# Eight PSUM banks in one rotation for two middle batches, and a new order of their output products and transpositions

## The chip, the cores and the metric

The kernel runs on one core of a Trainium2 chip. The metric is the time of one execution in microseconds on the device. The engines named below are TensorE (PE in the rows, PEld for its weight loads), VectorE (DVE), ScalarE (ACT), GpSimd (POOL) and the queue of DMA issues (SP).

## The reference

Three layers run one after another on 4 batches of 576 positions, all in fp32: windowed attention with 8 heads of 64, a gated MLP in which the gate mixes positions, and a gated convolutional MLP.

```python
scores = scale * q @ k.T;  scores = where(mask, scores + bias, -1e9)   # window of 128
attn = exp(scores - max);  x = (attn / sum(attn)) @ v                  # per head, then [B, S, 512]

h = gelu(x @ w_in);  u, v = split(h)
v_n = (v - mean(v)) / sqrt(var(v) + 1e-6) * g_ln
v_s = einsum('ts,bsd->btd', w_sg, v_n) + b_sg[:, None]
x = x + (u * v_s) @ w_out

h = relu(x @ w_in2);  conv = 3-tap convolution of h along the positions
out = (h * sigmoid(conv)) @ w_out2
```

## The kernel before

The whole kernel is one program in which every engine has its own queue and takes its instructions strictly in the order in which they stand there. `_steps()` writes the order of the work by hand as a list of short names, each one a step of one batch; a scheduler then places the instructions of these steps on the engines, mostly in that order, but it may move one up or down by its own estimate of time.

Attention for batch b + 1 is woven into the gated MLP of batch b. Attention works on pairs of heads, four to a batch (pair 1 of batch 2 is `2.1`). Its steps:

- `L`, `M` load a pair's k and q, and its v. `C` (line 464) computes the scores: 23 groups of matmuls into five PSUM banks named `sc`, and nine masking instructions on VectorE (line 451) that read them.
- `E` (line 489) is nine exponentials on ScalarE, and `N` (line 495) divides by the sums: nine multiplications, shared between VectorE and GpSimd (line 242).
- `T` (line 529) turns the weights with 13 transpositions into four banks named `pT`; four copies to SBUF (`ph`) follow, two on ScalarE and two on VectorE. The first transposition waits for the last masking instruction listed before it (line 533).
- `A` (line 585) forms the pair's products with v in two banks named `o`, 52 small matmuls. The first waits for all four copies (`s["waits"]`, line 538). `X` splits the result x into a high and a low part (`xg`).

The gated MLP's steps each take one bank: `V` (`psv`, line 746, five a batch), `U` (`psu`, line 787), `G` (`pss`, line 824) and `W` (`pso`, line 845). `U`, `G`, `W` are named by batch, half (256 or 320 positions) and a quarter of the columns. A `G` step goes on as: VectorE scales it (line 840), GpSimd multiplies by u, a copy makes the high part `gh`, a subtraction the low part `gl`. A `W` step is 12 matmuls over `gh` and `gl` of all four quarters; VectorE adds x (line 858) and a DMA writes the result. Steps `a` (line 382) narrow a piece of a later layer's weights: five instructions on VectorE that write `wa` (lines 324 to 331), two on GpSimd, and DMAs in and out.

PSUM has eight banks. Line 276 divides them:

```python
psum(net=2, att=6)
```

`bank(name)` (line 265) takes the next of two banks for names that begin with ps, and the next of six for the others. When a pool's banks are used up, the next step waits until the oldest tile of that pool has been read. The step `B` (line 866) makes one pool of all eight; the kernel before never runs it. Before batch 3 line 895 sets `psum(net=4)`.

Of the kernel before, what the change touches and what calls it, by code (L numbers as in the profile page):

```python
# [14 lines left out]
B, H, S, D = 4, 8, 576, 64  # L15
# [38 lines left out]
def _steps():  # L54


    def of(p):
        return f"{p // NP}.{p % NP}"

    def scores(p):  # L60
        return [f"C{of(p)}"]

    def weigh(p):
        return [f"E{of(p)}", f"N{of(p)}"]

    def back(p):
        return [f"T{of(p)}", f"A{of(p)}"]

    def halves(p):
        return [f"X{of(p)}.0", f"X{of(p)}.1"]  # L70

    def loads(p):
        return [f"L{of(p)}", f"M{of(p)}"]

    weave = lambda main, more: [
        x for i, m in enumerate(main) for x in [m] + more[i * len(more) // len(main) : (i + 1) * len(more) // len(main)]
    ]
    put_by = [f"a{i}.{c}" for i in (1, 0) for c in range(16)]
    s = """
        l0.0 k0 l1.0 k5 l2.0 l3.0 v0.0 v1.0 v2.0 v3.0 j1.0 j1.1 l0.1  # L80
        c0.0 e0.0 c1.0 e1.0 n0.0 c2.0 e2.0 t0.0 n1.0 c3.0 e3.0 l1.1 j1.2 j1.3 v0.1 i1.0 z0.0 X0.0.0 t1.0 n2.0 z1.0 X0.1.0
        l2.1 v1.1 i1.1 t2.0 n3.0 z2.0 X0.2.0 c0.1 e0.1 l3.1 j0.0 i1.2 t3.0 z3.0 X0.3.0 c1.1 e1.1 v2.1 i1.3 n0.1 c2.1 j0.1 v3.1 j0.2 t0.1 e2.1 n1.1 z0.1
        i0.0 c3.1 e3.1 j0.3 i0.1 k4 V0.0 t1.1 n2.1 z1.1 V0.1 t2.1 n3.1 z2.1 i0.2 U0.0.0 i0.3 t3.1 z3.1 X0.0.1 U0.0.1
        X0.1.1 U0.0.2 X0.2.1 X0.3.1
    """.split()
    for b in range(B - 1):
        p = NP * (b + 1)
        V = [f"V{b}.{j}" for j in range(5)]
        U = [[f"U{b}.{half}.{m}" for m in range(4)] for half in range(2)]
        G = [[f"G{b}.{half}.{m}" for m in range(4)] for half in range(2)]  # L90
        W = [[f"W{b}.{half}.{m}" for m in range(4)] for half in range(2)]
        if b == 0:
            uv = ["g0", "g1", V[2], "g2", "o0.0", U[0][3], "g3", "o0.1", V[4]] + loads(p) + ["g4", "o1.0"] + scores(p) + ["o1.1", V[3], "o2.0", "o2.1"]
            uv += loads(p + 1) + U[1][:2] + ["o3.0"] + scores(p + 1) + ["o3.1"] + loads(p + 2) + U[1][2:] + scores(p + 2)
        else:
            uv = V[:2] + loads(p) + scores(p) + V[2:] + loads(p + 1) + scores(p + 1) + U[0] + loads(p + 2) + U[1][:1] + scores(p + 2) + U[1][1:]
        T, A = ([f"{x}{of(p + i)}" for i in range(4)] for x in "TA")
        gw = weigh(p) + G[0] + weigh(p + 1) + G[1][:1] + loads(p + 3) + T[:1] + G[1][1:2] + W[0][:1] + A[:1] + halves(p)
        gw += weigh(p + 2) + W[0][1:2] + T[1:2] + W[0][2:] + A[1:2] + scores(p + 3) + halves(p + 1) + weigh(p + 3) + T[2:3] + G[1][2:3]
        gw += A[2:3] + halves(p + 2) + G[1][3:] + T[3:] + W[1][:1] + A[3:] + halves(p + 3) + W[1][1:]  # L100
        if b == 0:
            s += uv + gw
        else:
            now = put_by[10 * b - 10 : 10 * b]
            s += weave(uv, now[:4]) + weave(gw, now[4:])
    first = " ".join(s)
    n = [f"V3.{j}" for j in (0, 1, 2, 4, 3)] + [f"U3.{half}.{m}" for half in range(2) for m in range(4)]
    n += [f"G3.0.{m}" for m in range(4)] + ["G3.1.0"] + [f"W3.0.{m}" for m in range(4)]
    n += [f"G3.1.{m}" for m in range(1, 4)] + [f"W3.1.{m}" for m in range(4)]

    for m in range(4):
        n[n.index(f"U3.{m % 2}.{m // 2 + 1}")] += f" w0.{m // 2}.{m % 2}"
    n[n.index("W3.0.3")] += " y0.0"
    n[n.index("G3.1.2")] += " y0.1"
    n[n.index("W3.1.0")] += " y0.2"
    n[n.index("W3.1.1")] += " y0.3"
    s = weave(n[:-6], put_by[LATE:]) + n[-6:]
    late = [f"w1.{k}.{h}" for k in range(4) for h in range(2)]
    s = s[:-6] + weave(s[-6:], late)
    second = " ".join(["x0.0.1.2.3"] + s)  # L120
    return first, second


STEPS = _steps() + (
    """
    D0.0 D0.1 D0.2 D0.3 x1.0.1 D0.4 x1.2.3 D0.5 y1.0 D0.6 y1.1 D0.7 y1.2 y1.3 D1.0 D1.1 F0.0 D1.2 D1.3 F0.1 D1.4
# [989 lines left out]
```

## Time and profile before

| | us |
|---|---|
| median of 3 runs | 545.88 (544.20 to 546.34) |
| the profiled execution | 545.05 |
| its span | 543.2 |
| TensorE busy in the span | 522.3 (96%) |
| VectorE, ScalarE, GpSimd busy | 370.0 (68%), 258.6 (48%), 243.0 (45%) |
| batch 1 of the gated MLP (`V1.0` to the end of `W1.1.3`) | 126.10 to 205.50 |
| batch 2 | 205.50 to 284.91 |

The span begins with the first instruction and ends with the last; 1.85 us of the profiled execution lie around it. In a list in order of time, successive instructions of one kind are merged into one row, and the brackets at its end give the idle time before it and what ended it. [...]

### The profile page before, as it was taken

The page shows a single profiled execution, that of the slowest core. Times are in us where ns is not written, and L with a number is a line of the kernel's source. Part 1 is how long each engine was busy: PE and PEld are TensorE (multiplying, and loading weights), DVE is VectorE, ACT ScalarE, POOL GpSimd, SP SyncE. Part 2 cuts the span into 40 slices and gives each one's busy share as a digit, 9 for nine tenths or more (in the row PEclk, how much of TensorE's full clock was granted, in tenths as well). Part 3 has the DMA queues.
Part 4 walks back from the last instruction along what each step waited for, and adds up shares of the span by engine and source line. Part 5 has one row for each costly group of instructions (what it writes and reads, how often), then busy time and mean ns, then how long its engine had stood idle before and what let it go on. Part 6 is the DMA issues. An engine that isn't in the chain of part 4 may idle for free.

```text
span 543.2 us, 11985 instructions
## 1 busy us (share of the span) xinstructions
PE 522.3 (96%) x4548; PEld 474.8 (87%) x4548; DVE 370.0 (68%) x959; ACT 258.6 (48%) x673; POOL 243.0 (45%) x383
## 2 busy tenths in 40 slices
PE   8997989999999999999999999999999999999997
PEld 6776879898898888898988999998998999999887
DVE  4999898754869865869867788698467344654300
ACT  6694578342458451457544534453444334444311
POOL 2444249552246263237363354245586445465500
PEclk9999989999999999999999999999999999999999
DMA  8974441433260766240734424811202200100111
GB/s 298 385 241 172 150 126 45 146 120 106 80 194 21 229 183 198 68 136 24 241 124 131 154 80 155 306 43 43 83 21 69 77 21 19 42 21 22 37 39 59
DMA packets 33209, 63.93 MB, mean 118 GB/s; under 512 B 3968, under 2 KB 13952, under 8 KB 33152
## 3 DMA queue, kind: packets, MB, share of 16 engines
q1 hardware_dynamic: 33008, 63.04, 35.0%
q8 instruction: 36, 0.59, 0.4%
q14 instruction: 21, 0.17, 0.1%
q10 hardware_dynamic: 144, 0.13, 0.1%
HBM read 48.47 MB, written 14.68 MB: 116 GB/s over the span
## 4 chain that ended last, share of the span: by engine, by line
PE 57%; DVE 17%; ACT 11%; POOL 8%; DMA 3%; issue 3%; ACTq 0%; POOLq 0%; DVEq 0%; SPq 0%
PE psg L213 31%; PE pso L213 7%; PE psu L213 5%; ACT t L186 5%; PE psv L213 4%; PE o L213 3%; PE sc L213 3%; POOL t L242 3%; PE pss L213 3%; DVE t L451 2%; PE pT L515 2%; DMA x2d<-x 2%; DVE t L242 1%; DVE wa L330 1%; DVE wa L329 1%
## 5 line engine op out<-in xcount | busy, mean ns | idle before, releaser
L213 PEld LDWEIGHTS psg<-x2g,w 128*128 128x128 f32 x768 | 103.2, 188 | 2.4 <-ACT hb L970 0.7
L213 PE MATMUL psg<-x2g,w 128*128 128x256 f32 (+1 forms) x768 | 104.7, 294 | 0.6 <-ACT hb L970 0.5
L213 PE MATMUL psg<-wout,gh 128*128 128x512 f32 (+1 forms) x272 | 80.1, 378 | 0.0
L186 ACT ACTIVATE t<-t,st 128x192 f32<-128x192 f32 (+1 forms) x144 | 61.9, 431 | 16.6 <-DVE st L451 16.6
L213 PE MATMUL pss<-wsg,vn 128*128 128x256 f32 (+1 forms) x448 | 63.6, 299 | 0.3 <-DVE t L840 0.2
L213 PEld LDWEIGHTS pss<-wsg,vn 128*128 128x128 f32 x448 | 60.7, 191 | 1.2 <-DVE t L840 1.1
L974 DVE SCALAR_TENSOR_TENSOR cc<-hb,cw,cc 128x576 f32<-128x576 f32 x32 | 26.5, 832 | 47.0 <-POOL cc L242 47.0
L213 PEld LDWEIGHTS psg<-wout,gh 128*128 128x128 f32 x272 | 49.7, 188 | 8.7
L213 PE MATMUL psu<-xg,win 128*128 128x320 f32 (+1 forms) x384 | 54.4, 298 | 3.0 <-ACT win L222 1.7
L213 PEld LDWEIGHTS psu<-xg,win 128*128 128x128 f32 x384 | 51.6, 188 | 4.3 <-ACT win L222 1.8
L213 PE MATMUL pso<-gh,wo 128*128 128x256 f32 (+1 forms) x256 | 52.2, 300 | 1.7 <-DVE t L840 1.6
L213 PE MATMUL psg<-wout,gl 128*128 128x512 f32 (+1 forms) x136 | 50.9, 378 | 0.0
L213 PE MATMUL psv<-win,xg 128*128 128x512 f32 x192 | 47.6, 398 | 1.0 <-DVE wa L328 0.9
L242 POOL TENSOR_SCALAR cc<-hb,cw 128x576 f32<-128x576 f32 x32 | 28.4, 889 | 42.7 <-ACT hb L970 42.7
L451 DVE CUSTOM_DVE_ANT_0 t<-sc,tab 128x192 f32<-128x192 f32 (+1 forms) x144 | 40.3, 335 | 4.9 <-PE sc L213 4.9
L970 ACT ACTIVATE hb<-psg 128x576 f32<-128x576 f32 x32 | 20.7, 651 | 47.5 <-PE psg L213 45.1
L213 PEld LDWEIGHTS pso<-gh,wo 128*128 128x128 f32 x256 | 40.2, 188 | 3.4 <-DVE t L840 2.8
L213 PEld LDWEIGHTS psv<-win,xg 128*128 128x128 f32 x192 | 35.4, 188 | 8.9 <-ACT win L222 1.0
L231 DVE TENSOR_TENSOR gg<-cc,hb 128x576 f32<-128x576 f32 x32 | 30.2, 944 | 17.2 <-ACT cc L186 17.0
L213 PE MATMUL pso<-gl,wo 128*128 128x256 f32 (+1 forms) x128 | 36.9, 301 | 2.4 <-DVE gl L231 1.7
L231 POOL TENSOR_TENSOR t<-t,u 128x256 f32<-128x256 f32 (+1 forms) x32 | 27.0, 850 | 21.3 <-DVE t L840 20.3
L231 POOL TENSOR_TENSOR gl<-gg,gh 128x512 fp32r<-128x512 f32 x24 | 33.7, 1406 | 0.6
(101 smaller groups left out, 963.1 us busy)
## 6 DMA issues: line engine op xcount, KB each, us to landing
V<-in_v_dram SPq DMA_DIRECT2D x12, 704.0 KB, 5.1
x2s<-x2d SPq DMA_DIRECT2D x16, 288.0 KB, 2.9
w<-in_w_in_dram SPq DMA_DIRECT2D x8, 512.0 KB, 7.4
w<-in_w_out_dram SPq DMA_DIRECT2D x16, 256.0 KB, 2.9
w<-in_w_in_dram SPq DMA_DIRECT2D x16, 256.0 KB, 2.7
wout<-w2d SPq DMA_DIRECT2D x8, 512.0 KB, 6.1
q<-in_q_dram SPq DMA_DIRECT2D x12, 320.0 KB, 3.9
out_dram<-ot SPq DMA_DIRECT2D x15, 256.0 KB, 2.0
```

Source lines behind the costliest of these rows:

```text
L186: ins = nc.scalar.activation(*args, **kw)
L213: return nc.tensor.matmul(out, lhsT, rhs, start=start, stop=stop, **kw)
L231: return (nc.vector if eng == "dve" else nc.gpsimd).tensor_tensor(dst, a, b, op=op)
L242: e.tensor_scalar(dst, src, col, 1.0, op0=ALU.mult, op1=ALU.mult)
L329: nc.vector.tensor_scalar(a, a, 0x07FFFFFF, 3, op0=ALU.bitwise_and, op1=ALU.logical_shift_left)
L330: nc.vector.scalar_tensor_tensor(a, high, 0xC0000000, a, op0=ALU.bitwise_and, op1=ALU.bitwise_or)
L451: nc.vector.tensor_tensor_reduce(e, bank, table, scale=-SCALE, scalar=3e38, op0=ALU.add, op1=ALU.min, accum_out=mx)
L515: grouped(nc.tensor.transpose(ps[:, i * P : (i + 1) * P], src, ident), first and i == 0, waits if i == 0 else ())
L970: nc.scalar.activation(h[:, 1 : S + 1], ps[:, 256 : 256 + S], AF.Relu)
L974: nc.vector.scalar_tensor_tensor(cc, h[:, 0:S], cw[:, 0, c : c + 1], cc, op0=ALU.mult, op1=ALU.add)
```

## The change

After batch 0 the new step `B` joins the eight banks into one rotation, which serves attention and gated MLP alike in batches 1 and 2. In these two batches the list is also new from the exponentials on: the first output product `W.0.0` stands behind the first pair's `A` and `X` and the third pair's `E` and `N`; the third pair's transposition `T` stands ahead of the fourth pair's scores `C`; the last two products `G.1.2` and `G.1.3` and the fourth `W.0.3` come together behind the fourth pair's `E` and `N`.

```diff
--- before.py
+++ after.py
@@ -98,8 +98,12 @@
         gw = weigh(p) + G[0] + weigh(p + 1) + G[1][:1] + loads(p + 3) + T[:1] + G[1][1:2] + W[0][:1] + A[:1] + halves(p)
         gw += weigh(p + 2) + W[0][1:2] + T[1:2] + W[0][2:] + A[1:2] + scores(p + 3) + halves(p + 1) + weigh(p + 3) + T[2:3] + G[1][2:3]
         gw += A[2:3] + halves(p + 2) + G[1][3:] + T[3:] + W[1][:1] + A[3:] + halves(p + 3) + W[1][1:]
+        if b:
+            gw = weigh(p) + G[0] + weigh(p + 1) + G[1][:1] + loads(p + 3) + T[:1] + G[1][1:2] + A[:1] + halves(p)
+            gw += weigh(p + 2) + W[0][:1] + T[1:2] + W[0][1:2] + A[1:2] + halves(p + 1) + T[2:3] + W[0][2:3] + scores(p + 3)
+            gw += A[2:3] + halves(p + 2) + weigh(p + 3) + G[1][2:] + W[0][3:] + T[3:] + W[1][:1] + A[3:] + halves(p + 3) + W[1][1:]
         if b == 0:
-            s += uv + gw
+            s += uv + gw + ["B"]
         else:
             now = put_by[10 * b - 10 : 10 * b]
             s += weave(uv, now[:4]) + weave(gw, now[4:])
```

On TensorE the first place is the end of the last early product of the mixing matrix in batch 1. Before:

```order
L213 MATMUL pss_2547<-wsg0_851,vn_2065 128x320
L213 MATMUL pss_2547<-wsg0_851,vn_2095 128x320
L213 MATMUL pss_2547<-wsg1_852,vn_2095 128x320
L213 MATMUL pso_2569<-gh_2390,wo_891 128x256 x2
L213 MATMUL pso_2569<-gl_2391,wo_891 128x256
```

and now:

```order
L217 MATMUL pss_2552<-wsg0_851,vn_2070 128x320
L217 MATMUL pss_2552<-wsg0_851,vn_2100 128x320
L217 MATMUL pss_2552<-wsg1_852,vn_2100 128x320
L217 MATMUL o_2575<-ph_2549,V_1979 64x64 x4
L217 MATMUL o_2575<-ph_2542,V_1979 64x192
```

The 18 first matmuls of the two output products `pso` are gone from here; the first pair's products with v (`o`) follow `pss` directly.

The second place is behind these products, around the second pair's transposition. Before:

```order
L213 MATMUL o_2596<-ph_2537,V_1974 64x64
L213 MATMUL o_2596<-ph_2530,V_1974 64x64
L515 MATMUL pT_2672<-ident_80,t0_85 128x128 x4
L515 MATMUL pT_2679<-ident_80,t0_85 128x128 x4
L515 MATMUL pT_2686<-ident_80,t0_85 128x128 x4
L515 MATMUL pT_2693<-ident_80,t0_85 128x128
L213 MATMUL pso_2569<-gh_2456,wo_891 128x256 x2
L213 MATMUL pso_2569<-gl_2457,wo_891 128x256
```

and now:

```order
L217 MATMUL o_2585<-ph_2542,V_1979 64x64
L217 MATMUL o_2585<-ph_2535,V_1979 64x64
L217 MATMUL pso_2645<-gh_2395,wo_891 128x256
L519 MATMUL pT_2661<-ident_80,t0_85 128x128 x4
L519 MATMUL pT_2668<-ident_80,t0_85 128x128 x4
L519 MATMUL pT_2675<-ident_80,t0_85 128x128 x4
L519 MATMUL pT_2682<-ident_80,t0_85 128x128
L217 MATMUL pso_2645<-gh_2395,wo_891 128x256
```

One matmul of the first output product stands ahead of the transposition, and all others behind it.

On VectorE the place is in batch 2, between the third pair's division by the sums and the copies of the second pair's transposed weights (`ph`). Before:

```order
L242 TENSOR_SCALAR t2_87<-t2_87,r_3834 128x192 x4
L231 TENSOR_TENSOR gl_3647<-t1_3643,gh_3646 128x256
L224 CAST gh_3702<-t1_3699 128x320
L231 TENSOR_TENSOR xg_3819<-x_3775,xg_3819 128x256
L224 COPY ph_3863<-pT_3862 128x512
L224 COPY ph_3870<-pT_3869 128x512
L231 TENSOR_TENSOR xg_3822<-x_3775,xg_3822 128x320
```

and now:

```order
L246 TENSOR_SCALAR t2_87<-t2_87,r_3823 128x192 x4
L235 TENSOR_TENSOR gl_3652<-t1_3648,gh_3651 128x256
L228 CAST gh_3707<-t1_3704 128x320
L235 TENSOR_TENSOR xg_3795<-x_3764,xg_3795 128x256
L328 TENSOR_SCALAR wa_3800<-w64_3798 128x256
L332 TENSOR_SCALAR wa_3800<-wa_3800 128x256
L333 TENSOR_SCALAR wa_3800<-wa_3800 128x256
L334 SCALAR_TENSOR_TENSOR wa_3800<-w64_3798,wa_3800 128x256
L335 SCALAR_TENSOR_TENSOR wa_3800<-w64_3798,wa_3800 128x256
L235 TENSOR_TENSOR xg_3811<-x_3764,xg_3811 128x320
L228 COPY ph_3852<-pT_3851 128x512
L228 COPY ph_3859<-pT_3858 128x512
```

Five instructions of a narrowing step (`wa`) and both low parts of x (`xg`) now stand ahead of the two copies; before, one low part did. In batch 1 three of the five stand there.

## Rows read from the trace of the kernel before

**Rows 1.** Busy time by engine, two stretches (columns: length, busy us, instructions, clock, DMA)

```profile
169.79:205.50 35.71, 32.69 (x419) 30.38 (x418) 27.50 (x85) 17.46 (x53) 17.23 (x33) 1.00 0.59 180
...
250.40:284.91 34.51, 32.46 (x419) 30.46 (x418) 27.50 (x85) 17.48 (x53) 17.20 (x33) 1.00 0.47 151
```

**Rows 2.** TensorE in order of time, batch 1 (columns: start us, us, engine, line, operation)

```profile
169.79 0.41 PE L213 MATMUL pso<-gh,wo 128*128 128x256 f32 x2
...
173.44 2.05 PE L213 MATMUL o<-ph,V 128*64 128x64 f32 x52
...
175.41 1.64 PE L515 MATMUL pT<-ident,t 128*128 128x128 f32 x13
...
176.81 0.48 PE L213 MATMUL pso<-gh,wo 128*128 128x256 f32 x2
...
177.96 2.04 PE L213 MATMUL o<-ph,V 128*64 128x64 f32 x52 [0.21 <-ACT ph L222]
...
179.94 0.50 PE L213 MATMUL pso<-gh,wo 128*128 128x256 f32 x2
...
182.88 1.97 PE L213 MATMUL sc<-k,q 64*64 64x128 f32 x46
...
184.64 4.37 PE L213 MATMUL pss<-wsg,vn 128*128 128x320 f32 x28
...
201.89 0.55 PE L213 MATMUL pso<-gh,wo 128*128 128x320 f32 x2
```

**Rows 3.** TensorE in order of time, batch 2

```profile
205.50 5.68 PE L213 MATMUL psv<-win,xg 128*128 128x512 f32 x24
...
219.00 2.09 PE L213 MATMUL psv<-win,xt 128*128 128x512 f32 x8 [0.43 <-ACT v L186]
...
226.17 4.76 PE L213 MATMUL psu<-xg,win 128*128 128x256 f32 x36 [0.45 <-ACT u L186]
...
250.40 0.40 PE L213 MATMUL pso<-gh,wo 128*128 128x256 f32 x2
...
284.91 8.40 PE L213 MATMUL psv<-win,xg 128*128 128x512 f32 x36
```

**Rows 4.** ScalarE in order of time, first pair's copies in batches 1 and 2

```profile
171.14 1.04 ACT L222 COPY ph<-pT 128x512 f32<-128x512 f32 x2
...
251.76 1.05 ACT L222 COPY ph<-pT 128x512 f32<-128x512 f32 x2
```

**Rows 5.** VectorE in order of time, batches 1 and 2

```profile
172.38 1.07 DVE L330 SCALAR_TENSOR_TENSOR wa<-w,wa 128x256 uint32<-128x256 uint32 x1
...
197.52 1.02 DVE L231 TENSOR_TENSOR gl<-t,gh 128x320 fp32r<-128x320 f32 x1 [2.68 <-ACT gh L222]
...
237.86 0.29 DVE L324 TENSOR_SCALAR wa<-w 128x256 uint32<-128x256 uint32 x1
...
239.30 0.42 DVE L331 SCALAR_TENSOR_TENSOR wa<-w,wa 128x256 uint32<-128x256 uint32 x1
...
254.45 1.59 DVE L242 TENSOR_SCALAR t<-t,r 128x192 f32<-128x192 f32 x4
...
257.20 1.28 DVE L224 COPY ph<-pT 128x512 f32<-128x512 f32 x2
```

**Rows 6.** GpSimd in order of time, batch 1

```profile
172.30 0.88 POOL L231 TENSOR_TENSOR t<-t,u 128x320 f32<-128x320 f32 x1 [2.05 <-DVE t L840]
...
191.62 3.71 POOL L242 TENSOR_SCALAR t<-t,r 128x128 f32<-128x128 f32 x8 [0.73 <-DVE r L499]
```

**Rows 7.** TensorE in order of time, the wait before 76.79

```profile
76.79 2.20 PE L213 MATMUL sc<-k,q 64*64 64x192 f32 x24 [2.08 <-DVE st L451]
```

**Rows 8.** Busy time by engine in two-microsecond stretches behind that wait

```profile
76.00:78.00 2.00, 1.21 (x23) 1.13 (x23) 2.00 (x15) 2.00 (x10) 0.00 (x0) 0.79 0.75 291
...
78.00:80.00 2.00, 2.00 (x10) 2.00 (x9) 1.97 (x8) 2.00 (x10) 0.14 (x1) 0.50 0.04 8
...
80.00:82.00 2.00, 2.00 (x17) 2.00 (x16) 2.00 (x17) 2.00 (x10) 1.35 (x2) 0.86 0.82 240
```

## The prediction

> **What bounds the kernel now.** I read the busy shares first. TensorE works 96% of the span, so only its waits can be won. The change touches batches 1 and 2, and in each the list is new only behind the six early `pss` products, from 169.79 to 205.50 and from 250.40 to 284.91. [...]
>
> Then I took TensorE in order of time and worked out what each kind of work takes from start to start [rows 2]: a pair's products with v 1.97 us (173.44 to 175.41), its transpositions 1.40 (175.41 to 176.81), 24 `pso` matmuls of 256 columns 2.94 (179.94 to 182.88), so 0.1225 each and 1.47 for a step of 12, the scores 1.76 (182.88 to 184.64), two `pss` steps 4.37 by their own row; 24 `pso` matmuls of 320 columns from 201.89 to `psv` at 205.50 [rows 2, 3] 3.61, so 0.150 each. The stretch holds 4 products with v, 3 transpositions, 4 + 4 `pso` steps, one set of scores and two `pss` steps: 7.88 + 4.20 + 5.88 + 7.22 + 1.76 + 4.37 = 31.31 us. So before waits 4.4 us in batch 1 and 3.2 in batch 2, with the pipeline's small gaps in it. This is nearly all the change can win.
>
> **The change part by part.** The work itself stays: the same matmuls, copies and DMAs. What moves is order and banks.
>
> *Banks in the steps V and U.* In batch 1 TensorE does not wait for a bank there. In batch 2 it waits 0.43 us at 219.00 for an activation that reads `psv` and 0.45 at 226.17 for one that reads `psu` [rows 3], each the tile two before in a pool of two. In a rotation of eight the tile before was read long ago. These 0.88 us go, and ScalarE's chain of exponentials starts as much earlier, because it hangs on the last `psu`. Bounds: 0, if VectorE, whose order is unchanged, holds the later steps back, and 0.88. I take 0.88, since ScalarE's copies set the next start.
>
> *The first pair's products ahead of the first `pso`.* Before, 18 `pso` matmuls stand between `pss` and these products. Now nothing does, but the products wait for all four copies of the transposed weights. ScalarE's two stand behind the third pair's exponentials and end at 171.14 + 1.04 = 172.18 and at 251.76 + 1.05 = 252.81 [rows 4]; TensorE can start some 0.1 later, at 172.28 and 252.91. So TensorE stands idle for about 2.5 us, from 169.79 and from 250.40, where before it had `pso` to do. The products begin 1.2 us earlier than before (173.44), but with 18 matmuls (2.2 us) still owed.
>
> *Up to the second pair's products.* Batch 1: 172.28 + 1.97 + 0.12 (one `pso` matmul) + 1.40 = 175.77; the other 23 take 2.82, to 178.59. Then the second pair's products wait for copies on VectorE. In batch 2 that queue reads, before: four normalizations (from 254.45, 1.59, to 256.04), 1.16 us for a low part, a cast and a subtraction, then the two copies from 257.20 for 1.28 [rows 5]. Now a fifth normalization of 128 columns stands there (an estimate of 0.3, from 1.59 / 4 for 192), and behind the same 1.16 come five narrowing instructions (237.86 to 239.30 + 0.42, so 1.86 [rows 5]) and the second low part of x (an estimate of 0.39, a third of the 1.16). The copies end at 256.34 + 1.16 + 1.86 + 0.39 + 1.28 = 261.03, and TensorE starts at 261.1. It was ready at 252.91 + 1.97 + 0.12 + 1.40 + 22 x 0.1225 = 259.1, so it waits 2.0. In batch 1 (80.6 us earlier) three of the five stand in front, 1.12 us: copies end at 179.65, products start at 179.75, a wait of 1.16. At this point the new order has done the same work as before but stands at 179.75 where before stood at 177.96 [rows 2].
>
> What hides beside a neighbour is not certain here. A narrowing instruction took 1.07 us at 172.38 instead of 0.42 while GpSimd multiplied from 172.30 for 0.88 [rows 5, 6]. So each batch's queue may be 0.65 later where such a pair meets, which I keep for the range. [...]
>
> *Scores and third transposition.* The third pair's transposition now stands ahead of the fourth pair's scores and so no longer waits for their masking. Batch 1 goes on without a wait: 179.75 + 1.97 + 1.40 + 1.47 + 1.76 + 1.97 = 188.32, where the two `pss` steps start; they end 4.37 later, at 192.69. Batch 2: 261.1 + 1.97 + 1.40 + 13 x 0.1225 + 1.76 + 1.97 = 269.79, and 274.16.
>
> *The last products.* The `pso` steps of the second half need the low part of the fourth `pss`. Before, the two `pss` steps ended at 184.64 + 4.37 = 189.01 [rows 2], and this low part at 197.52 + 1.02 = 198.54 [rows 5]: 9.53 us for scaling, multiplication, cast and subtraction, of which GpSimd's eight normalizations took 3.71 [rows 6]. Now they stand ahead of that multiplication on GpSimd and mostly beside `pss`. I take 9.53 - 3.71 = 5.82 (bounds: 4.0, as a guess below, since scaling, 0.88 us of multiplication, cast and subtraction must run in turn and two copies stand between, and 9.53). The fourth pair's copies stand just ahead of this subtraction on VectorE, so its products start at 192.69 + 5.82 + 0.1 = 198.6 and, in batch 2, at 280.1. Behind them 37 matmuls of 0.150 are left: 198.6 + 1.97 + 5.55 = 206.1, and 287.6.
>
> So batch 1 ends 0.6 us later than 205.50, batch 2 loses 287.6 - 284.91 = 2.7 less the 0.88. *Banks and queues that cost nothing:* I followed the rotation: each tile eight before is read by then, except the scores of batch 2, whose first bank is freed by an addition behind two copies (0 to 0.35; I take 0). On SP two output writes of a batch come later, and behind them loads of weights that are due 5 us afterwards. Batch 3 and the last layer keep their order up to one `psg` step and are TensorE's.
>
> **Sum.** 545.05 - 0.88 + 0.6 + 2.7 = 547.5 us against the profiled execution's own time, which is 0.83 under the median shown (545.88): 0.3% above that median. I leave the difference between the two out, since the runs spread over 2.1 us. About 0.5% (2.7 us) is what a measurement of this kernel can tell from no change.
>
> **The rivals.**
>
> *The clock falls behind the new waits (slower).* [...] I give this rival 0.27.
>
> *The copies come early after all (faster).* If VectorE's and GpSimd's queues run ahead of my estimates, only the first wait of 2.5 stays, and each stretch takes 31.31 + 2.5 = 33.8: 1.9 and 0.7 less than before, with the 0.88 some 3.5, so 541.6. For it: VectorE has 7 to 8 us free in each stretch [rows 1]. Against it: free time lies elsewhere than ahead of the copies, and the queue is fixed. 0.15.
>
> *The change does not do what it says.* The banks free nothing, since the 0.88 us come back as waits for data, and the moved steps cancel within 1 us: 546.0 to 548.4. 0.10.
>
> **How the numbers follow.** The forecast has 0.48: 547.5, its own range from 543.9 (both last chains at their lower bound, 1.8 less each) to 549.2 (0.65 more for each batch, and the 0.35). Of it 0.10 lie above 548.6 (slower by over 0.5% of the median). With the clock's 0.22 of 0.27 above that and 0.02 of the third, slower is 0.34; faster is 0.14, nearly all from the second rival; within 0.5% is 0.52. The range for 8 in 10 is 543.2 to 550.6.
>
> **What would show it.** In the changed kernel's profile TensorE should stand idle for about 2.5 us ahead of the first `o` in both batches, with ScalarE's copy as what ends it; 1 to 2 us ahead of the second, ended by a copy on VectorE; no wait at the third transposition and none for a bank in batch 2's steps V and U; and some 3 us around the first `pso` step of 320 columns. If the two stretches end under 35 us, my VectorE queue is wrong; if the clock row shows 0.5 there, the first rival is at work.

## The result and the profile after

The changed kernel took 552.35 us (median of 6 runs, 551.47 to 555.08) and the kernel before 546.11 us beside it (6 runs): a ratio of 1.0122 between the means, with a 95% interval of 1.0087 to 1.0158. It is 1.2% slower. The prediction was 547.5 us, with a range up to 550.6; the time lies above it. Medians and ratios here and below leave out a run over 1.5% slower than the fastest of its kernel, which is one run of e17 (558.89 us). The profiled execution of the changed kernel took 554.40 us, its span 552.6.

The first reading compares the kernels by batch. The rows give busy time by engine from the first `psv` of a batch to the first of the next, and for batch 3 to the first `psg` (columns: stretch, its length, then busy us and instructions of PE, PEld, DVE, ACT and POOL, the granted clock, DMA share and GB/s). Before:

```profile
126.10:205.50 79.40, 76.31 (x806) 70.31 (x805) 60.09 (x203) 38.95 (x120) 33.49 (x64) 1.00 0.44 135
205.50:284.91 79.41, 76.41 (x806) 70.20 (x805) 61.68 (x208) 38.84 (x120) 34.55 (x67) 1.00 0.40 127
284.91:334.50 49.59, 49.18 (x333) 46.15 (x331) 39.69 (x93) 20.78 (x49) 20.29 (x31) 1.00 0.42 130
```

After:

```profile
127.07:208.15 81.08, 77.41 (x806) 71.66 (x805) 64.82 (x210) 37.98 (x117) 31.12 (x58) 0.98 0.44 131
208.15:290.62 82.47, 76.22 (x806) 70.21 (x805) 66.61 (x215) 37.87 (x117) 33.28 (x63) 1.00 0.40 122
290.62:343.68 53.06, 49.99 (x332) 46.34 (x331) 39.63 (x92) 20.09 (x47) 20.28 (x32) 1.00 0.40 122
```

Batch 1 lost 1.68 us, batch 2 3.06 and batch 3, whose code did not change, 3.47. Another 0.97 us were lost ahead of batch 1, where both kernels are the same, and 0.22 behind the first `psg`; together 9.40, the difference of the spans. The 0.97 is this execution's own: in e17, the changed kernel once more, batch 1 begins at 125.87 us. VectorE is busy 4.7 to 4.9 us longer in batches 1 and 2, GpSimd 2.4 and 1.3 us less: four of a batch's 36 normalizations went from GpSimd to VectorE.

The stretches of [rows 1], from the end of the six early `pss` products (same columns), and TensorE in them, which answers to [rows 2, 3] (columns: start us, us, engine, line, operation, and in brackets the idle time before it and what ended it):

```profile
170.57:208.15 37.58, 33.91 (x418) 31.89 (x418) 32.43 (x92) 16.68 (x50) 15.08 (x27) 0.95 0.57 168
252.10:290.62 38.52, 32.50 (x418) 30.49 (x418) 32.17 (x92) 16.24 (x48) 15.60 (x28) 1.00 0.44 131
```

```profile
221.06 1.99 PE L217 MATMUL psv<-win,xt 128*128 128x512 f32 x8
...
173.19 3.19 PE L217 MATMUL o<-ph,V 128*64 128x64 f32 x52 [2.62 <-ACT ph L226]
...
181.08 2.04 PE L217 MATMUL o<-ph,V 128*64 128x64 f32 x52
...
189.92 4.38 PE L217 MATMUL pss<-wsg,vn 128*128 128x320 f32 x28
...
198.30 0.41 PE L217 MATMUL pso<-gl,wo 128*128 128x320 f32 x1 [0.38 <-DVE gl L235]
...
200.65 2.05 PE L217 MATMUL o<-ph,V 128*64 128x64 f32 x52
...
254.28 2.05 PE L217 MATMUL o<-ph,V 128*64 128x64 f32 x52 [2.18 <-DVE wa L332]
...
263.46 2.04 PE L217 MATMUL o<-ph,V 128*64 128x64 f32 x52 [2.81 <-issue]
...
272.42 4.37 PE L217 MATMUL pss<-wsg,vn 128*128 128x320 f32 x28
...
283.12 2.05 PE L217 MATMUL o<-ph,V 128*64 128x64 f32 x52
```

The stretches grew by 1.87 and 4.01 us. The foretold wait ahead of pair 0's products is there in both. In batch 1 the group behind it took 3.19 us instead of 2.05: the granted clock fell, as behind the wait of [rows 7, 8] (two-microsecond stretches, same columns):

```profile
172.00:174.00 2.00, 0.81 (x16) 0.76 (x18) 2.00 (x7) 1.45 (x5) 0.74 (x1) 0.95 0.00 0
174.00:176.00 2.00, 2.00 (x40) 2.00 (x38) 2.00 (x7) 0.37 (x1) 1.42 (x5) 0.50 0.10 12
176.00:178.00 2.00, 2.00 (x17) 1.88 (x14) 2.00 (x5) 0.89 (x2) 2.00 (x5) 0.70 0.56 175
```

The copies of [rows 4] stand where the prediction had them: ScalarE's end at 172.10 + 1.04 and 253.18 + 1.04, each just ahead of the products. (In batch 2 the trace names a narrowing instruction as what ended the wait, which ended 0.02 us behind the copies; the products do not read what it writes.)

```profile
172.10 1.04 ACT L226 COPY ph<-pT 128x512 f32<-128x512 f32 x2
...
253.18 1.04 ACT L226 COPY ph<-pT 128x512 f32<-128x512 f32 x2
```

The second pair's copies in batch 2 (VectorE in order of time; compare [rows 5]) stand behind five narrowing instructions (the last at 261.33) and a subtraction, and end at 263.36, 0.1 us ahead of the products at 263.46. The trace calls that wait "issue", a wait for nothing that it shows; by the kernel's `s["waits"]` the copies are what it waited for.

```profile
259.03 0.95 DVE L235 TENSOR_TENSOR xg<-x,xg 128x256 fp32r<-128x256 f32 x1
...
261.33 0.42 DVE L335 SCALAR_TENSOR_TENSOR wa<-w,wa 128x256 uint32<-128x256 uint32 x1
261.68 0.48 DVE L235 TENSOR_TENSOR xg<-x,xg 128x320 fp32r<-128x320 f32 x1
262.08 1.28 DVE L228 COPY ph<-pT 128x512 f32<-128x512 f32 x2
```

While the first of these subtractions ran, GpSimd worked on the narrowing too:

```profile
258.89 0.80 POOL L235 TENSOR_TENSOR wa<-wa,wh 128x256 fp32r<-128x256 f32 x1
```

In batch 3 TensorE waited three times for low parts from VectorE; before, once. The first row is the kernel before, the others the changed kernel:

```profile
322.88 0.61 PE L213 MATMUL pso<-gl,wo 128*128 128x256 f32 x3 [0.41 <-DVE gl L231]
...
326.03 0.39 PE L217 MATMUL pso<-gl,wo 128*128 128x256 f32 x1 [0.64 <-DVE gl L235]
328.70 0.38 PE L217 MATMUL pso<-gl,wo 128*128 128x256 f32 x1 [2.00 <-DVE gl L235]
332.05 0.62 PE L217 MATMUL pso<-gl,wo 128*128 128x256 f32 x3 [0.41 <-DVE gl L235]
```

Following that back leads through VectorE's narrowing pieces and ScalarE's to weight loads that were issued late, and from there to GpSimd at the start of the batch, in the kernel before and after (GpSimd in order of time):

```profile
283.97 0.57 POOL L225 TENSOR_SCALAR xt<-xg 128x128 fp32r<-128x128 f32 x2
286.45 0.30 POOL L225 TENSOR_SCALAR xt<-xg 128x128 fp32r<-128x128 f32 x1 [1.91 <-DVE wa L329]
288.63 0.30 POOL L225 TENSOR_SCALAR xt<-xg 128x128 fp32r<-128x128 f32 x1 [1.88 <-ACT v L186]
...
290.21 0.19 POOL L781 TENSOR_SCALAR rs<-ba 128x1 f32<-128x1 f32 x1
```

```profile
289.14 0.30 POOL L229 TENSOR_SCALAR xt<-xg 128x128 fp32r<-128x128 f32 x1 [2.45 <-DMA x2d<-x]
291.41 0.30 POOL L229 TENSOR_SCALAR xt<-xg 128x128 fp32r<-128x128 f32 x1 [1.97 <-DVE x L235]
294.03 0.30 POOL L229 TENSOR_SCALAR xt<-xg 128x128 fp32r<-128x128 f32 x1 [2.32 <-DMA x2d<-x]
296.02 0.30 POOL L229 TENSOR_SCALAR xt<-xg 128x128 fp32r<-128x128 f32 x1 [1.69 <-DMA x2d<-x]
...
297.60 0.19 POOL L785 TENSOR_SCALAR rs<-ba 128x1 f32<-128x1 f32 x1
```

`xt` is a small copy of x's tails. Its four tiles come from the group `t1` of four buffers, which also holds the `pso` results (`x2`) until they are stored. With the new list the last four `pso` steps follow one another, and GpSimd waits for stores ahead of the copies, three times by the trace's own naming. The last of the four stores is issued 0.72 us behind the batch's first `psv` in both kernels; it landed 2.8 us after that before the change, and 4.5 us after it here. Measured from the batch's first `psv`, the last `xt` starts at 5.40 us instead of 3.72, and behind it, in GpSimd's queue, the first norm (`rs`) at 6.98 instead of 5.30.

### The profile page after: what moved, and what is told of

Same layout as the page of the kernel before. It is cut to its first block, busy times and chain, and to the rows that moved or that the text cites. A ratio compares the mean times of both kernels' runs of the same rounds, so it can differ in the third digit from the quotient of the medians.

```text
span 552.6 us, 11993 instructions
## 1 busy us (share of the span) xinstructions
PE 525.0 (95%) x4548; PEld 477.5 (86%) x4548; DVE 379.3 (69%) x973; ACT 256.5 (46%) x667; POOL 239.1 (43%) x375
## 4 chain that ended last, share of the span: by engine, by line
PE 58%; DVE 15%; ACT 9%; POOL 7%; DMA 5%; issue 4%; SPq 0%; ACTq 0%; POOLq 0%; DVEq 0%
PE psg L217 31%; PE pso L217 6%; PE psv L217 5%; PE psu L217 5%; ACT t L190 5%; PE o L217 4%; PE sc L217 3%; PE pT L519 2%; POOL t L246 2%; DMA x2d<-x 2%; DMA w<-in_w_in_dram 2%; DVE t L455 2%; PE pss L217 2%; DVE wa L332 1%; DVE wa L334 1%
```

## The experiments

Times are medians, ratios against the kernel before in the same session; before took 545.4 to 546.4 us there. b1 to b3 are the batches as above, in each kernel's profiled execution, and "falls" the falls of the granted clock to 0.50 in them (one that lasts twice as long counts as two). The code of the edits is shortened; `...` stands for what is left out.

| kernel | us | ratio (95%) | b1 | b2 | b3 | falls |
|---|---|---|---|---|---|---|
| before | | | 79.40 | 79.41 | 49.59 | 0 |
| after | 552.35 | 1.0122 (1.0087–1.0158) | 81.08 | 82.47 | 53.06 | 1 |
| e1 rotation, old list | 560.60 | 1.0259 (1.0218–1.0301) | 83.71 | 84.40 | 51.42 | 3 |
| e2 new list, two pools | 549.51 | 1.0069 (1.0043–1.0094) | 80.58 | 81.28 | 52.22 | 1 |
| e3 new list in batch 2 only | 558.48 | 1.0222 (1.0189–1.0256) | 83.95 | 83.55 | 51.40 | 2 |
| e4 first `pso` first | 553.88 | 1.0142 (1.0096–1.0188) | 80.85 | 81.44 | 50.92 | 0 |
| e5 narrowing earlier | 562.35 | 1.0284 (1.0246–1.0323) | 85.88 | 85.23 | 51.55 | 4 |
| e6 clock held | 553.55 | 1.0119 (1.0088–1.0151) | 80.98 | 81.44 | 51.23 | 0 |
| e7 rotation, old list, one move | 558.24 | 1.0221 (1.0188–1.0254) | 83.14 | 84.37 | 50.88 | 1 |
| e8 two pools, one move | 548.38 | 1.0039 (1.0016–1.0063) | 80.46 | 79.46 | 49.80 | 0 |
| e9 `xt` apart | 549.68 | 1.0079 (1.0048–1.0109) | 81.08 | 82.48 | 49.53 | 2 |
| e11 pools reopened | 546.44 | 0.9997 (0.9973–1.0021) | 79.36 | 79.71 | 50.14 | 0 |
| e12 copies on ScalarE | 550.89 | 1.0088 (1.0060–1.0116) | 82.65 | 80.84 | 49.93 | 3 |
| e13 three edits | 550.49 | 1.0080 (1.0051–1.0108) | 80.16 | 81.58 | 49.86 | 1 |
| e14 e9 and e12 | 550.86 | 1.0084 (1.0052–1.0116) | 81.03 | 81.15 | 49.63 | 2 |
| e15 e14, clock held | 547.74 | 1.0035 (1.0011–1.0059) | 79.50 | 79.53 | 49.68 | 0 |
| e16 before, `xt` apart | 543.63 | 0.9958 (0.9935–0.9980) | 78.86 | 78.21 | 49.88 | 0 |
| e17 after again | 552.77 | 1.0130 (1.0083–1.0176) | 82.65 | 81.88 | 51.80 | 3 |

**The two halves of the change apart (e1, e2, e3, e11).** The edits against the changed kernel:

```diff
# e1: rotation, old list                # e3: the same with "if b == 2:"
-        if b:
+        if b == 9:
# e2: new list, two pools
-            s += uv + gw + ["B"]
+            s += uv + gw
# e11: as e1, and
-        psum(all=8)
+        psum(net=2, att=6)
```

e1: 

> The step B alone: eight banks in one rotation for batches 1 to 3, the list gw of the kernel before. Theory 1 (the order of the list costs, the rotation gives about 1 us): no wait at the start of batch 2's psv and psu products, pair 0's products directly behind the first pso in both batches with a wait under 0.5 us, 544 to 546.5 us, ratio 0.996 to 1.001. Rival (the rotation costs, because products and transpositions now take their bank behind copies of the network's): 550 us or more, ratio over 1.007. On batch 3, which was 3.5 us longer in the changed kernel's profiled run: if the rotation brings that, psv to psg of batch 3 takes 52 to 53 us here, otherwise 49.5 to 50.

e2: 

> The new list in batches 1 and 2, without the step B: two banks for the network's products and six for attention, as before. Theory 1: the idle times ahead of pair 0's products (2.2 to 2.6 us per batch) stand, the bank waits at psv and psu of batch 2 (0.4 us each) come back: 552 to 555 us, ratio 1.010 to 1.017. Rival (the rotation costs): 545 to 548 us, ratio under 1.004.

e3: 

> Rotation kept, the new list in batch 2 only, the old one in batch 1. Theory 1: batch 1 back at 35.7 to 36 us from the last pss ahead of the first products to batch 2's first psv, so about 2 us less than the changed kernel: 549.5 to 551 us, ratio 1.006 to 1.010. If the loss in batch 3 follows the list of batch 2 it stays (52 to 53 us from psv to psg). If it follows a clock that fell in batch 1, it goes: 547 us.

e11: 

> A control: the list of the kernel before; the step B closes the two pools behind batch 0 and opens them again with the same two and six banks. If closing and opening the pools is part of what the rotation cost with the old list (560.6 us): 548 us or more. If sharing the banks is all of it: 544.5 to 546.5 us. The waits at batch 2's psv and psu (0.43 and 0.45 us before): there, if the banks make them.

My theory had the sign of the rotation wrong. With the old list it costs about 15 us; closing and opening the pools costs nothing (e11), so the sharing does it. The largest single wait is at the third pair's transpositions. They wait for the fourth pair's masking, and before, with `pss` in banks of its own, 28 `pss` matmuls stood between the scores and them. In e1 the scores (184.86) are followed at once by the transpositions, which wait 4.07 us (the last mask ends at 190.75; the trace names an exponential that came with it):

```profile
184.86 1.97 PE L217 MATMUL sc<-k,q 64*64 64x128 f32 x46
190.90 3.01 PE L519 MATMUL pT<-ident,t 128*128 128x128 f32 x13 [4.07 <-ACT t L190]
193.56 2.59 PE L217 MATMUL pss<-wsg,vn 128*128 128x320 f32 x14
```

The new list, which puts the transpositions ahead of the scores, gives most of this back: 552 us with both. Without the rotation it still costs 0.7%, but not by the wait that was foretold: with two pools the scheduler puts the first `pso` ahead of the first pair's products again, and TensorE waits 0.64 us there, as before the change. So e2 is not the changed kernel's order with other banks; banks and list together make the order. e3's miss follows: its batch 1 has the old list under the rotation.

**One move alone (e7, e8).** In the old list:

```diff
-... A[1:2] + scores(p + 3) + halves(p + 1) + weigh(p + 3) + T[2:3] + ...
+... A[1:2] + (T[2:3] if b else []) + scores(p + 3) + halves(p + 1) + weigh(p + 3) + ([] if b else T[2:3]) + ...
```

e7: 

> One rotation of eight banks with the old list, where the list differs in one place: the third pair's transpositions stand ahead of the fourth pair's scores in batches 1 and 2. The rotation with the old list took 560.6 us, and its profile shows the third pair's transpositions waiting 4.07 and 4.00 us for the fourth pair's masks, with the clock at half behind each. Theory D (that wait, and what hangs on it, is the rotation's price): both waits gone, no fall of the clock there, 547 to 551 us. Rival (the rotation costs at other places too, as products that come round to banks held by scores): 555 us or more.

e8: 

> The kernel before with the same one move (third pair's transpositions ahead of the fourth pair's scores) and its two pools of two and six banks. Before shows 0.62 us ahead of the third pair's transpositions in batch 1 and none in batch 2. Theory D: the move is worth only that wait, 544.5 to 546 us, no change that can be told. Rival (the move costs what the new list costs, because the fourth pair's scores and all behind them start later): 548 to 550 us.

Theory D fell. The two waits are gone in e7, but it gained only some 2 us, with intervals that overlap; in their place stand a wait of 1.31 us at a `pss`, for a copy of attention's weights (`ph`), and several under 1.1. Under the rotation the old list is slow at more than one place, and I did not take these apart further. e8 shows that the move costs about 0.4% even with two pools.

**Inside the new list (e4, e5, e6, e12).**

```diff
# e4
-... G[1][1:2] + A[:1] + halves(p)  / weigh(p + 2) + W[0][:1] + T[1:2] ...
+... G[1][1:2] + W[0][:1] + A[:1] + halves(p)  / weigh(p + 2) + T[1:2] ...
# e5
-            s += weave(uv, now[:4]) + weave(gw, now[4:])
+            s += weave(uv, now[:7]) + weave(gw, now[7:])
# e6, in product(), ahead of a waiting group; the first real product overwrites the bank
+        for n in range(held):          # 9 for pairs (2, 0), (3, 0) and (3, 1)
+            nc.tensor.matmul(o, tab[:, 0, :P], tab[:, 0, :512], start=True, stop=True)
# e12, in a_transpose()
+            second = b >= 2 and m == 1
-            pc, p1 = turned(...), turned(...);  last = pick(...)
+            pc, p1 = turned(..., "act" if second else "act dve"), ...;  last = "act" if second else pick(...)
```

e4: 

> The changed kernel with one edit: the first pso of each batch (1.8 us of matmuls) stands ahead of pair 0's products again, as in the kernel before; the rest of the new list stays (third pair's transpositions ahead of the fourth's scores, fourth pair's weights behind). Theory 1 in its narrow form (the idle time ahead of pair 0's products is the cost): about 1.8 us back per batch, and no fall of the clock behind it: 546 to 548.5 us. Theory 1 in its wide form (what is queued ahead of the second pair's copies on VectorE, and the late start of the rest, cost as much): the second pair's wait of 2 to 3 us in batch 2 stays, 549 to 551 us. Rival (rotation): 552 us, no change.

e5: 

> The changed kernel; of the ten pieces that narrow second-stage weights in batches 1 and 2, seven instead of four are woven into the V and U stretch and three instead of six into the G and W stretch. Theory A (VectorE's queue: pieces ahead of the second pair's copies cost batch 2 its wait of 2.8 us, and pieces that end late in batch 2 hold the weight loads of batch 3 back, 2.6 us of idle time there): batch 2's second pair waits under 1 us, batch 3's first weight load is issued by 5.6 us behind its first psv instead of 7.3, batch 3 takes 50 instead of 53 us, in all 547.5 to 549.5 us. Theory B (the waits come from the order on TensorE and the banks alone, the pieces only fill idle time): 551 to 553 us, batch 3 at 52 to 53. Rival: V and U stretches, where VectorE has the layer norms, get longer by what G and W gain: 551 us or more.

e6: 

> The changed kernel with nine dummy products (bf16, 128 by 512, results overwritten) directly ahead of the products that waited 2.62, 2.18 and 2.81 us: pair 0's in batches 1 and 2 and the second pair's in batch 2. They wait for nothing and take some 1.9 us of each wait, so TensorE isn't idle there; what the products wait for is unchanged. If falls of the granted clock behind these waits carry a good part of the loss (theory C): mean clock up from 0.988 towards 0.995, pair 0's o group 2.05 us in place of 3.19 in batch 1, 548 to 550 us. If not (the waits themselves are the cost): 552 to 553 us at the same or a higher mean clock.

e12: 

> The changed kernel with all four copies of the second pair's transposed weights on ScalarE in batches 1 and 2 (two of them were on VectorE, behind five narrowing instructions and a subtraction, while ScalarE sat idle for 6 us). Theory F (VectorE's queue ahead of these copies makes the second pair's wait): no wait of over 0.4 us ahead of the second pair's products in either batch, 2.5 us back in batch 2 and up to 1.2 in batch 1, 548.5 to 550 us. Rival (the time is bound further on, at the fourth pair, by the chain from pss to the last low part): the wait goes and comes back later, 551.5 us or more.

e4 gives nothing that can be told from the changed kernel: the first pair's wait is gone, but the first `pso` waits 0.96 and 1.07 us and the second pair 1.58 and 1.60. Theory A fell: with pieces moved forward, the first transpositions wait 6.95 and 6.03 us for normalizations on GpSimd, and batch 3's first load stays at 7.1 us. e6 is the clearest reading on the clock. Two of its timed runs, one of them the profiled one, had a mean clock of 1.000 and took 552.09 and 551.57 us; in the other four it was 0.988 to 0.993, so there the clock fell somewhere all the same. In batch 1 the products start at the same distance from `psv` (46.12 us) as in the changed kernel and take 2.05 instead of 3.19, but then the second pair waits 1.21 us that it did not wait there:

```profile
172.67 2.05 PE L219 MATMUL o<-ph,V 128*64 128x64 f32 x52 [0.66 <-ACT ph L231]
...
180.28 1.93 PE L219 MATMUL o<-ph,V 128*64 128x64 f32 x48 [1.21 <-issue]
```

So theory C's 548 to 550 us did not come: in this pair of executions, what the fall cost was swallowed. It rests on two runs without a fall, and e17 below has a second fall that cost time. e12 takes that second wait away, as theory F said, and came out between the two forecasts: batch 2 shorter by 1.6 us, but batch 1 longer, with two falls in it that nothing swallowed.

**Batch 3 (e9, e17) and what is left (e13, e14, e15).**

```diff
# e9, in m_v(), the tail's step
-            xt = [mpool.tile([P, 320], F32R, tag="t1", name="xt", bufs=NT1)[:, :P] for _ in range(NK)]
+            if b == B - 1:
+                xt = [mpool.tile([P, 320], F32R, tag="gt", name="xt", bufs=NGT)[:, :P] for _ in range(NK)]
+            else: ...                  # as before
# e13: e4, e9 and e12 together          # e14: e9 and e12
# e15: e14 and nine dummy products for pairs (2, 0) and (3, 0)
```

e9: 

> The changed kernel; in batch 3 the four copies xt of x's tails are written to buffers of the gt group instead of those that the last pso results (x2) are stored from, so GpSimd doesn't wait for their stores. In the changed kernel the last four pso follow one another, their four stores are issued in 4.9 us, and GpSimd makes its last xt copy 5.4 us behind batch 3's first psv (before: 3.7), the first norm and the first weight load of batch 3 following at 7.0 and 7.3 (before: 5.3 and 5.6). Theory E (this chain is batch 3's loss): last xt by 2.5 us, first norm by 5.0, batch 3 takes 49.5 to 50.5 us from psv to psg instead of 51 to 53, 549.5 to 551 us. Rival (batch 3's loss comes from VectorE's narrowing pieces, whatever GpSimd does): 552 to 553 us, idle time of 1.5 us or more ahead of the first pso of batch 3.

e17: 

> The changed kernel again, unaltered, beside the three others on one chip: 551.5 to 553 us, batches 1 and 2 at 81.1 and 82.5 us whether the clock falls in them or not, batch 3 at 52 to 53 us with GpSimd's last xt copy 5 us or more behind its first psv. If the 3.5 us of batch 3 were a matter of the one execution that was profiled, batch 3 takes under 50.5 us here.

e13: 

> The changed kernel with three edits at once: the first pso ahead of pair 0's products, the second pair's copies all on ScalarE, and xt in batch 3 in buffers of its own. If each part is worth what its theory says (1.5, 3.0 and 1.5 to 2.5 us): 545 to 547 us, level with the kernel before. If the parts swallow each other, because the same later waits take up what they give: 549 us or more.

e14: 

> The changed kernel with the two edits that each gave something: the second pair's copies all on ScalarE, and batch 3's xt in buffers of the gt group. By the profiles, batch 3 is then 49.5 us; batches 1 and 2 have no second wait left, and what is above the kernel before (79.4 us each) is 1.7 us for each fall of the clock behind the waits of 2.6 us ahead of pair 0's products: 81.0 each with one fall, in all 548.5 to 550.5 us. If the two gains are one and the same (batch 3's xt is early as soon as batch 2's pso end earlier): 550.5 to 551.5 us.

e15: 

> The same with nine dummy products (bf16, 128 by 512) ahead of pair 0's products in batches 1 and 2, inside the waits of 2.62 us, so that TensorE isn't idle there. In the changed kernel holding the clock gave nothing, since the second pair's wait swallowed what a fall cost. Theory G (with that wait gone, the falls are what remains of the loss): batches 1 and 2 at 79 to 79.7 us each, 545 to 547 us, level with the kernel before. Rival (the chain to the fourth pair bounds these batches whatever the clock): 81 us each, 549 us or more.

Theory E held. In e9 the three `xt` copies behind the last `pso` go at once, the batch takes 49.53 us as before the change, with batches 1 and 2 unchanged to 0.01 us:

```profile
288.13 0.82 POOL L229 TENSOR_SCALAR xt<-xg 128x128 fp32r<-128x128 f32 x3 [2.73 <-PE pso L217]
294.52 0.19 POOL L788 TENSOR_SCALAR rs<-ba 128x1 f32<-128x1 f32 x1 [1.38 <-DVE ba L786]
```

e17 shows the loss again in another execution: last `xt` at 5.24 us, batch 3 at 51.80. It missed on batch 1: 82.65 us, since a second fall came, from about 199.5 us on, behind small waits of 0.37 and 0.36 us at 197 and 198 (the fourth pair's products took 3.63 us at 199.43, and 2.04 in batch 2), where nothing swallowed it. In e14 the gain of e12 and that of e9 do not add up: batch 3 is already short in e12's profile (49.93 us). Its last four stores are issued at the same distances from `psv` as in the changed kernel, to 0.01 us, but the last one landed after 2.9 us and not 4.5 (4.4 in e17), and the last `xt` starts 3.79 us behind `psv` (the trace names a VectorE instruction as its releaser; the store landed 0.2 us before). So the loss in batch 3 hangs on when the stores land, which the list alone does not fix; what made them land sooner in e12 stays open. The rows of e12 and e17:

```profile
293.57 0.30 POOL L229 TENSOR_SCALAR xt<-xg 128x128 fp32r<-128x128 f32 x1 [0.86 <-DVE cw L896]
...
295.64 0.30 POOL L229 TENSOR_SCALAR xt<-xg 128x128 fp32r<-128x128 f32 x1 [3.05 <-DMA x2d<-x]
```

The 18 profiles agree: where the last `xt` starts at most 3.9 us behind `psv`, batch 3 takes 49.5 to 50.1 us; where it starts at 4.1 us or later, 50.9 to 53.1, though not in proportion. e13 came out as its second case, with 550.49 us: its three edits do not add up either.

Then e15 against e14: with the second pair's wait gone, the same dummy products that gave nothing in e6 give 3.1 us, and all three batches are back to within 0.12 us of before. The timed 0.35% that remains was not traced to a place.

```profile
127.03:206.53 79.50, 77.72 (x814) 70.95 (x814) 62.48 (x207) 39.13 (x120) 31.02 (x58) 1.00 0.45 134
206.53:286.06 79.53, 77.76 (x814) 71.00 (x814) 63.98 (x212) 39.13 (x120) 33.87 (x66) 1.00 0.41 127
286.06:335.74 49.68, 49.26 (x332) 46.22 (x331) 39.24 (x92) 20.65 (x47) 19.29 (x29) 1.00 0.41 127
```

**A faster kernel (e16).** Before, with `xt` in the `gt` group in batches 1 to 3 (`if b:` in place of `if b == B - 1:`).

e16: 

> The kernel before, with xt in buffers of the gt group in batches 1 to 3. There GpSimd's last xt copy stands 3.7 us behind batch 3's first psv, and TensorE waits 0.43 and 0.45 us at psv and psu of batch 2 and 0.41 us at the first pso of batch 3. If GpSimd's wait for the stores makes these (the norms of V stand behind it): 544 to 545 us, ratio 0.996 to 0.999. If the banks make them: no change, 545 to 546.5 us, waits as before.

It beats both, 543.63 us. Batches 1 and 2 are 0.5 and 1.2 us shorter:

```profile
126.21:205.07 78.86, 76.06 (x806) 70.15 (x805) 60.23 (x203) 38.93 (x120) 33.41 (x64) 1.00 0.45 136
205.07:283.28 78.21, 75.97 (x806) 70.27 (x805) 62.04 (x208) 38.91 (x120) 34.55 (x66) 1.00 0.42 130
```

In the kernel before, GpSimd's last `xt` copies of batch 2 stood at 210.01, 4.5 us behind the first `psv`; now all are done before it, the norms come 1.9 us earlier, and the waits of [rows 3] at `psv` and `psu` are gone, with two pools. So these waits began on GpSimd. A wider rotation of banks hid them; this removes their cause. Batch 3 gained nothing: it takes 49.88 us, and its first `pso` still waits 0.42.

## Why the prediction was wrong

The step that failed is "Banks and queues that cost nothing". It noted that on SP "two output writes of a batch come later, and behind them loads of weights that are due 5 us afterwards", and that batch 3 keeps its order and is TensorE's. The order was kept, but I followed the later writes only along SP's queue and not into the buffers that they free. GpSimd's `xt` waits for those, and its norm and the loads wait behind `xt`. The term, 0 in the sum, measured 3.47 us in the profiled execution and 2.2 in e17; undoing it alone gave 0.43% (1.0122 to 1.0079, two sessions, with intervals that overlap), and batch 3 back to 49.53. What the prediction left out is the time that a store takes to land: the last one is issued at the same distance from `psv` as before, lands 1.7 us later, and holds `xt` until then. In e12's profile the same list ran without this delay.

The other steps, term by term:

- *Banks in V and U of batch 2*: -0.88 predicted; 44.90 us from `psv` to the end of the early `pss` became 43.95, so -0.95. Right: `xt` was late in the changed kernel too (4.9 us), and the eight banks hid it.
- *First pair's products*: right. Idle 2.62 and 2.18 us for 2.5, ended by ScalarE's copies.
- *Up to the second pair*: right in kind, too small in batch 2. The products were forecast 8.19 us behind pair 0's and came at 9.18. Behind pair 0's products, VectorE's normalizations began 0.55 us later than forecast. Then the low part, the cast and the subtraction took 1.85 us for 1.16: the subtraction alone took 0.95 (259.03), while GpSimd worked (258.89, for 0.80); one of the same shape took 0.42 at 265.29. The prediction kept 0.65 us for such a pair in its range, from a narrowing instruction; the five narrowing instructions took 1.78 for 1.86. In batch 1 the clock's fall took the place of the forecast wait; e6 has that wait, 1.21 us for 1.16 (the prediction's own terms, added up again, give 1.19).
- *Third pair*: right, no wait in either batch.
- *The last products*: 5.9 us from the end of `pss` to the products were forecast, 6.35 and 6.33 measured, and from the second pair's products to `pss` 0.27 more than forecast in each batch.
- So batch 1's stretch lost 1.87 us for 0.6 and batch 2's 4.01 for 2.7. These 2.6 us by themselves would have left the sum inside the range (550.1); with batch 3's loss it is not. In e17 the shares differ: batch 1 lost 3.25 us, with two falls of the clock, batch 2 2.47 and batch 3 2.21.
- Some 2 us of the profiled execution's time are its own: 554.40 against a median of 552.35.

The rivals: falls of the clock did come behind the new waits, as the first rival said (a fall to 0.50 in batch 1; in e9 and e17 in both), but the two runs of e6 without a fall took as long as the changed kernel. The falls are not the main cause there, though a second one cost batch 1 of e17 1.57 us, and they become a cause when the second pair no longer waits (e14, e15). The changed kernel's timed runs have mean clocks of 0.984 to 0.994; what the falls carry in the medians is not shown. Not every long wait brought a fall: 2.18 and 2.81 us in batch 2 passed at 1.00. The chance of 0.27 for this rival was the author's estimate, and no run had shown what a fall costs; in the runs it was 1.53 and 1.62 us where nothing swallowed it (e14 against e15), and nothing in batch 1 of the changed kernel against e6. The faster rival was out: neither pair's copies came early. That the change does nothing fell with the ratio. None of the rivals had batch 3 in it.

What stays open is why the rotation with the old list costs 15 us, of which the third pair's wait explains only a part, and why the same stores land after 2.9 us in one execution and after 4.5 in another.

## What to carry to other kernels

When instructions at the end of a stage move, follow each one past its own queue to the buffer that it frees, through to the store that lands: whoever takes that buffer next, on any engine, is moved too, and all that is queued behind it (here GpSimd's last `xt`, 5.40 us behind `psv` instead of 3.72). Two streams of work that share one rotation of banks wait for each other's readers (in e7 a `pss` waited 1.31 us for attention's copy), so a shared rotation and the order under it are one change; run each half alone before judging either, and read what order the scheduler then makes. A fall of the clock cost time here only where no later wait swallowed it: holding the clock gave nothing in e6, where the second pair still waited 1.21 us, and 3.1 us in e15, where that wait was gone. So it is worth trying after the waits are gone, not before.

## What the hardware showed that was not expected

Each single fall of the granted clock read in these profiles was alike: the time below 1.00, each stretch taken by what its clock is short of 1.00, adds up to 1.70 to 1.72 us of lost full-speed time, as in the rows from 172 to 178 (0.10 + 1.00 + 0.60) and in [rows 8] (0.42 + 1.00 + 0.28). Where nothing swallowed it, it took 1.53 and 1.62 us of real time (e14 against e15, batches 1 and 2), and none where the next wait did (batch 1 of the changed kernel, 81.08 with a fall, against e6, 80.98 without). In the profiled executions of e6 and e15 dummy bf16 products filled the long waits (1.89 us of them in batch 1 of each, with 0.66 and 0.67 us idle behind), and the granted clock stayed at 1.00 through batches 1 to 3. In the changed kernel waits without work went both ways: behind 2.62 us in batch 1 the clock fell to 0.50, and 2.18 and 2.81 us in batch 2 passed at 1.00. So an idle stretch does not bring a fall each time.

Equal stores can take different times to land. The stores here are followed by loads of 288 KB of the same data. In the kernel before, the last four stores of batch 2 are issued within 5.5 us, with a median of 1.9 us from issue to landing; in the changed kernel within 4.2 us, with a median of 3.7. Being close together is not all of it: with the same issue times the median was 3.0 in e12 and in e17. Before (columns: operation, count, size of each, median us to landing):

```profile
x2d<-x SPq DMA_DIRECT2D x4, 160.0 KB, 1.9
```

After:

```profile
x2d<-x SPq DMA_DIRECT2D x4, 160.0 KB, 3.7
```
